# Splitting the attention result straight out of PSUM, in a kernel of linear attention and two MLPs

## The chip, the cores and the metric

The kernel runs on one core of a Trainium2 chip. The metric is the device time of one execution, in microseconds; the median of several executions counts. Times in the profile are those of one execution that the hardware profiler recorded.

## What is computed

An attention with a decaying state runs over 4 sequences of 768 steps, with 8 heads of 48 dimensions. Its output, as 3072 tokens of 384 numbers, goes through two MLPs of 2048 hidden units. The first has a clamped square as its activation, the second a sigmoid gate.

```python
for t in range(S):
    cur = np.einsum('bhd,bhe->bhde', u[None] * kt, vt)
    y[:, :, t] = np.einsum('bhd,bhde->bhe', rt, state + cur)
    state = wt[:, :, :, None] * state + np.einsum('bhd,bhe->bhde', kt, vt)
x = y.transpose(0, 2, 1, 3).reshape(B * S, H * D)

h = x @ w_in                                   # first MLP
g = np.where(h >= 1, h, np.where(h <= -1, 0.0, (h + 1) ** 2 / 4))
x = g @ w_out
h = x @ w2_in                                  # second MLP
out = (h / (1.0 + np.exp(-1.702 * h))) @ w2_out
```

## The kernel before

**Attention.** The 3072 tokens are cut into 24 windows of 128. `window(n)` is a generator that issues one window's instructions in about a dozen pieces, with a `yield` between them. A window loads its inputs (`rk`, `rkn`, `vn`, `lt`), runs two scans of the decay on VectorE (L433 and L435), multiplies and masks on GpSimd, ScalarE and VectorE, and does four groups of small matmuls: the transposes `tp`, the scores `sc`, the state `kv` and the result `yt`. At its end ScalarE copies the result `yt` from PSUM into `xr` in SBUF (L533). The four heads' pairs stand in four column blocks; six small DMAs (L536) move pieces of the fourth block into unused partitions of the other three, so that three blocks of 128 rows are left. Then ScalarE rounds `xr` into `xh` (L547), and VectorE (first six windows) or GpSimd (the other eighteen) forms the rest, `xl = xr - xh` (L550). `xr` has one buffer.

**MLPs.** Eight token tiles of 384, three windows each, go through the first MLP and then the second. One step `f` of a tile does nine matmuls of 128x384 into `hp` (L664: three of `xh` by `whi`, three of `xl` by `whi`, three of `xh` by `wlo`), the activation, and, three steps later, nine matmuls into three accumulators `acc` (L673, in the second MLP L682). Sixteen steps make a tile. The activation of the first MLP is three instructions: VectorE clamps `hp` to -1..1 (L701), ScalarE squares (L702), VectorE takes the maximum with `hp` (L714). ScalarE then rounds to `gh` (L695), and GpSimd or VectorE forms `gl` (L689).

**Weights.** They arrive as 64-bit numbers, in 32 pieces for the first MLP (`wst`, four buffers). Each piece costs two VectorE instructions (`ct` in PSUM, then `wt`), a ScalarE conversion (`wb`), an addition on GpSimd, a rounding on ScalarE (`whi`) and, from the eleventh piece on, a subtraction for `wlo` (L177), in turn on VectorE and GpSimd. The first ten pieces are converted before the first step.

**What sets the order.** Everything up to the end of the first tile (16 steps) is put in order by a scheduler, which may run an instruction earlier than it is written if it has a higher rank. The conversions inside the first tile are issued under `hooks["prio"](CP1)`, which gives them the rank `CP1`. From the second tile on, the order is the one in which the code is written: each step calls the attention's generators in turn, so that the windows of the next tile are spread over the steps of this one. A window whose last yielded value is `"x"` is held until its tile is at most one ahead of the tile that is running. Before, that yield stood ahead of the rounding into `xh`. DMAs are issued by SyncE (SP), in order.

The names that matter below: `xr`, `xh`, `xl` and the lines L533 to L550; `relu2_a` (L701, L702), `relu2_b` (L714); `split_x2`, which makes the second MLP's `xh` and `xl`; `ALT`, the choice of the activation's form in the first `ALT_N` tiles; `CP1`.

Of the kernel before, what the change touches and what calls it, by code (L numbers as in the profile page):

```python
# [9 lines left out]
F32 = mybir.dt.float32  # L10
F32R = mybir.dt.float32r
# [11 lines left out]
W = 128  # L23
# [15 lines left out]
TN = 384  # L39
# [12 lines left out]
LO0 = 'p'  # L52
LO1 = 'dg'
PUT = 1
ALT = (0,)
ALT_N = 1
N0 = 10
PRIO = True
# [4 lines left out]
F0 = 0  # L63
WP0 = 400
CP0 = 300
CP1 = 3000
MAXW = 6
GAP1 = 8
CHECK_LATE = True
# [30 lines left out]
def fast_path(st, tc, rkw_t, nat, v_l, w1, w2, u, out, x2_d, w2_d, flag_i, force):  # L100
# [121 lines left out]
            nc.scalar.activation(out=whi[f][q], in_=wf, func=AF.Copy)  # L222
            late.append((i, wf))

    xh, xl = {}, {}
    x2_t = {}
    accs = {}
    gq = {}
# [17 lines left out]

    def split_x2(i):
        x2 = x2_t.pop(i)
        h_ = p2.tile([128, KD, TN], F32R, tag="xh", name="x2h")
        l_ = p2.tile([128, KD, TN], F32R, tag="xl", name="x2l")  # L250
        nc.vector.tensor_copy(h_, x2)
        nc.vector.tensor_tensor(out=l_, in0=x2, in1=h_.bitcast(F32), op=ALU.subtract)
        xh[1, i], xl[1, i] = h_, l_
# [15 lines left out]
    def step(s):  # L269
        if s < NS:  # L270
            l, i, f, t0, n = where(s)
            last = l == 0 and i == len(TILES) - 1
            slots = l == 0 and not last
            if l == 0 and f == 0:
                cur[0] = i
            if l == 0 and i == 0:
                with hooks["prio"](CP1):
                    while nconv[0] < min(NPC, 2 * f + 2 + AHEAD):
                        conv_w1()
                    if nconv[0] == NPC:  # L280
                        conv_w1()
            hp = pools["h"][s % len(pools["h"])].tile([128, 512], F32, tag="h", name="hp")
            gemm1(nc, hp, n, xh[l, i], xl[l, i], f, win, whi, wlo)
            if l == 0 and ALT[f % len(ALT)] and i < ALT_N:
                t = relu2_c(nc, p2, hp, n, (None, nc.gpsimd, nc.vector)[ALT[f % len(ALT)]])
            else:
                t = (relu2_a, swish_a)[l](nc, p2, hp, n)
        if s - 1 in gq:
# [61 lines left out]
    with ExitStack() as sa:  # L350
# [65 lines left out]
        def window(n):  # L416
# [80 lines left out]
            yield from idle(GAPS[1])  # L497
            if PUT == 2 and not first:
                put(carry.pop())
            kvt = ps_s.tile([128, NC2, NP, D], F32, tag="s", name="kv")  # L500
            kv = [kvt[:, c] for c in range(1 if last else NC2)]

# [26 lines left out]
                carry.append(upd(1))  # L529
            yield from idle(GAPS[2])  # L530
            mm_y(1)
            xr = a2.tile([128, NP, W], F32, tag="xr", name="xr", bufs=1)
            nc.scalar.activation(out=xr, in_=yt, func=AF.Copy)  # L533
            for hh in range(2):
                for q in range(3):
                    nc.sync.dma_start(out=xr[64 * hh + D:64 * hh + 64, q, :], in_=xr[64 * hh + 16 * q:64 * hh + 16 * q + 16, 3, :])  # L536
            yield
            sq = vn.rearrange("p m h d -> p (m h d)")
            nc.scalar.activation(out=sq, in_=sq, func=AF.Square, accum_out=stat[:, n, 2:3])
            if n + 2 < NW:  # L540
                load_v(n + 2)
            yield "x"
            if off == 0:
                xh[0, ti] = p2.tile([128, KD, TN], F32R, tag="xh", name="xh")
                xl[0, ti] = p2.tile([128, KD, TN], F32R, tag="xl", name="xl")
            o = xh[0, ti][:, :, off:off + W]
            nc.scalar.activation(out=o, in_=xr[:, 0:KD, :], func=AF.Copy)  # L547
            if n >= XL_N:
                yield
            (nc.vector if n < XL_N else nc.gpsimd).tensor_tensor(out=xl[0, ti][:, :, off:off + W], in0=xr[:, 0:KD, :], in1=o.bitcast(F32), op=ALU.subtract)  # L550
            yield

        def idle(n):
# [152 lines left out]
def relu2_c(nc, p2, hp, n, eng):  # L706
    t = p2.tile([128, TN], F32, tag="t", name="t", bufs=3)
    nc.scalar.activation(out=t[:, 0:n], in_=hp[:, 0:n], func=AF.Relu, bias=0.5, scale=0.5)
    eng.scalar_tensor_tensor(out=t[:, 0:n], in0=t[:, 0:n], scalar=1.0, in1=t[:, 0:n], op0=ALU.min, op1=ALU.mult)
    return t  # L710


# [166 lines left out]
```

## Time and profile before

| what | value |
|---|---|
| median of 3 executions | 1003.78 us (1003.73 to 1005.83) |
| profiled execution, its own time | 1002.71 us |
| span from its first to its last instruction | 1001.0 us |
| PE busy | 945.8 us (94%) |
| VectorE (DVE) busy | 562.0 us (56%) |
| ScalarE (ACT) busy | 538.2 us (54%) |
| GpSimd (POOL) busy | 393.4 us (39%) |

The shares are means over stages that differ. In forty slices of the span, PE is at 4 to 6 tenths in the first four and at nine from the fifth on, while VectorE is at nine in the third, fourth and fifth slice. So the table has to be read together with a table by stage, which is what the first group of rows below is. Durations of neighbouring instructions on one engine overlap by some hundredths of a microsecond, so where many follow each other it is their distance from start to start that adds up.

### The profile page before, as it was taken

The page shows a single profiled execution, that of the slowest core. Times are in us where ns is not written, and L with a number is a line of the kernel's source. Part 1 is how long each engine was busy: PE and PEld are TensorE (multiplying, and loading weights), DVE is VectorE, ACT ScalarE, POOL GpSimd, SP SyncE. Part 2 cuts the span into 40 slices and gives each one's busy share as a digit, 9 for nine tenths or more (in the row PEclk, how much of TensorE's full clock was granted, in tenths as well). Part 3 has the DMA queues.
Part 4 walks back from the last instruction along what each step waited for, and adds up shares of the span by engine and source line. Part 5 has one row for each costly group of instructions (what it writes and reads, how often), then busy time and mean ns, then how long its engine had stood idle before and what let it go on. Part 6 is the DMA issues. An engine that isn't in the chain of part 4 may idle for free.

```text
span 1001.0 us, 18691 instructions
## 1 busy us (share of the span) xinstructions
PE 945.8 (94%) x6976; PEld 906.6 (91%) x6976; DVE 562.0 (56%) x983; ACT 538.2 (54%) x1279; POOL 393.4 (39%) x416
## 2 busy tenths in 40 slices
PE   4656999999999999999999999999999999999997
PEld 2445889999999999999999999999999999999997
DVE  6899976776877767777745753323232323232321
ACT  4666545666666667665654565555455433333332
POOL 6788744555555456455432541111111111111111
PEclk8857999999999999999999999999999999999999
DMA  9886515445555445553203443322222101000000
GB/s 236 208 226 176 140 24 164 132 118 140 156 134 147 117 113 154 144 146 104 66 20 115 129 133 99 96 78 85 87 81 85 59 2 45 3 28 22 25 1 28
DMA packets 52228, 101.73 MB, mean 102 GB/s; under 512 B 8608, under 2 KB 31392, under 8 KB 52128
## 3 DMA queue, kind: packets, MB, share of 16 engines
q1 hardware_dynamic: 52128, 100.45, 35.8%
q8 instruction: 57, 0.93, 0.4%
q14 instruction: 43, 0.35, 0.1%
HBM read 83.51 MB, written 15.73 MB: 99 GB/s over the span
## 4 chain that ended last, share of the span: by engine, by line
PE 63%; DVE 13%; ACT 10%; DMA 5%; issue 5%; SPq 3%; POOL 0%; ACTq 0%; DVEq 0%
PE hp L664 29%; PE acc L682 20%; PE acc L673 10%; SPq L536 3%; DVE pi L433 2%; DMA rk<-rkw_t 2%; DMA xr<-xr 2%; ACT gh L695 2%; DVE t L714 2%; ACT ra L472 2%; DVE ra L489 2%; ACT t L702 2%; DVE pi L435 1%; PE kv L508 1%; PE yt L514 1%
## 5 line engine op out<-in xcount | busy, mean ns | idle before, releaser
L689 POOL TENSOR_TENSOR gl<-t,gh 128x384 fp32r<-128x384 f32 x128 | 132.5, 1035 | 497.0 <-ACT gh L695 465.5
L695 ACT ACTIVATE gh<-t 128x384 fp32r<-128x384 f32 x256 | 134.1, 524 | 171.6 <-DVE t L714 93.4
L725 DVE TENSOR_TENSOR t<-t,hp 128x384 f32<-128x384 f32 x128 | 70.9, 554 | 218.6 <-ACT t L720 218.1
L720 ACT ACTIVATE t<-hp 128x384 f32<-128x384 f32 x128 | 62.8, 491 | 145.8 <-PE hp L664 145.8
L673 PE MATMUL acc<-gl,whi 128*128 128x384 f32 x384 | 131.2, 342 | 2.5 <-DVE gl L689 2.5
L673 PE MATMUL acc<-gh,whi 128*128 128x384 f32 x384 | 131.7, 351 | 0.8 <-ACT ev L263 0.3
L673 PE MATMUL acc<-gh,wlo 128*128 128x384 f32 x384 | 130.2, 339 | 0.0
L682 PE MATMUL acc<-wlo,gh 128*128 128x384 f32 x384 | 129.7, 338 | 0.0
L682 PE MATMUL acc<-whi,gh 128*128 128x384 f32 x384 | 129.5, 337 | 0.0
L682 PE MATMUL acc<-whi,gl 128*128 128x384 f32 x384 | 129.3, 337 | 0.0
L689 DVE TENSOR_TENSOR gl<-t,gh 128x384 fp32r<-128x384 f32 x128 | 75.4, 589 | 63.5 <-ACT gh L695 62.8
L702 ACT ACTIVATE t<-t 128x384 f32<-128x384 f32 x128 | 66.4, 519 | 65.7 <-DVE t L701 65.4
L714 DVE TENSOR_TENSOR t<-t,hp 128x384 f32<-128x384 f32 x128 | 70.2, 548 | 54.0 <-ACT t L702 52.5
L664 PE MATMUL hp<-xh,whi 128*128 128x384 f32 x384 | 91.9, 348 | 3.2 <-DVE t L714 3.2
L664 PE MATMUL hp<-xl,whi 128*128 128x384 f32 x384 | 89.3, 341 | 5.0 <-DVE xl L550 5.0
L701 DVE TENSOR_SCALAR t<-hp 128x384 f32<-128x384 f32 x128 | 70.4, 550 | 39.9 <-PE hp L664 39.6
L664 PE MATMUL hp<-x2h,whi 128*128 128x384 f32 x384 | 88.8, 339 | 0.0
L664 PE MATMUL hp<-xh,wlo 128*128 128x384 f32 x384 | 88.7, 339 | 0.0
L664 PE MATMUL hp<-x2l,whi 128*128 128x384 f32 x384 | 88.5, 339 | 0.0
L664 PE MATMUL hp<-x2h,wlo 128*128 128x384 f32 x384 | 88.1, 337 | 0.0
L673 PEld LDWEIGHTS acc<-gh,whi 128*128 128x128 f32 x384 | 72.2, 189 | 5.0 <-ACT ev L263 2.3
L673 PEld LDWEIGHTS acc<-gl,whi 128*128 128x128 f32 x384 | 72.6, 189 | 3.0 <-DVE gl L689 2.6
(108 smaller groups left out, 1849.1 us busy)
## 6 DMA issues: line engine op xcount, KB each, us to landing
wst<-w SPq DMA_DIRECT2D x96, 384.0 KB, 3.3
rk<-rkw_t SPq DMA_DIRECT2D x48, 288.9 KB, 5.0
rkn<-nat SPq DMA_DIRECT2D x24, 384.0 KB, 4.8
lt<-v_l SPq DMA_DIRECT2D x48, 128.0 KB, 3.7
w_d<-wt SPq DMA_DIRECT2D x32, 192.0 KB, 4.3
w2f<-w_d SPq DMA_DIRECT2D x32, 192.0 KB, 2.5
vn<-nat SPq DMA_DIRECT2D x24, 192.0 KB, 3.4
x_d<-ev SPq DMA_DIRECT2D x24, 192.0 KB, 2.2
```

What stands on the lines that cost most here:

```text
L433: nc.vector.tensor_tensor_scan(out=rr[:, WW:0:-1], data0=ws[:, WW:0:-1], data1=one_s[:, WW:0:-1], initial=0.0, op0=ALU.mult, op1=ALU.max)
L536: nc.sync.dma_start(out=xr[64 * hh + D:64 * hh + 64, q, :], in_=xr[64 * hh + 16 * q:64 * hh + 16 * q + 16, 3, :])
L664: nc.tensor.matmul(out=hp[:, 0:n], lhsT=win(a, f, kk), rhs=b[:, kk, 0:n], start=(i == 0), stop=(i == 3 * KD - 1))
L673: nc.tensor.matmul(out=acc[j][:, 0:n], lhsT=wout(a, f, j * 128, 128), rhs=b[:, 0:n], start=(f == 0 and i == 0), stop=(f == KF - 1 and i == 2))
L682: nc.tensor.matmul(out=o[:, 0:DM], lhsT=a[:, j * 128:(j + 1) * 128], rhs=wout(b, f, 0, DM), start=(f == 0 and i == 0), stop=(f == KF - 1 a ...
L689: eng.tensor_tensor(out=gl[:, 0:n], in0=t[:, 0:n], in1=gh[:, 0:n].bitcast(F32), op=ALU.subtract)
L695: nc.scalar.activation(out=gh[:, 0:n], in_=t[:, 0:n], func=AF.Copy)
L701: nc.vector.tensor_scalar(t[:, 0:n], hp[:, 0:n], scalar1=-1.0, scalar2=1.0, op0=ALU.max, op1=ALU.min)
L702: nc.scalar.activation(out=t[:, 0:n], in_=t[:, 0:n], func=AF.Square, bias=0.5, scale=0.5)
L714: nc.vector.tensor_tensor(out=t[:, 0:n], in0=t[:, 0:n], in1=hp[:, 0:n], op=ALU.max)
L720: nc.scalar.activation(out=t[:, 0:n], in_=hp[:, 0:n], func=AF.Sigmoid, scale=1.702)
L725: nc.vector.tensor_tensor(out=t[:, 0:n], in0=t[:, 0:n], in1=hp[:, 0:n], op=ALU.mult)
```

## The change

The window no longer has `xr`. ScalarE copies `yt` from PSUM directly into the rounded half of a joint tile `xx`, all four column blocks of it, and VectorE subtracts that half from `yt`, still in PSUM, into the other half. The six small DMAs then move both halves at once. The rounding and the subtraction that stood behind them are gone, for all windows. The yield of `"x"` moves up, ahead of the `kv` matmuls. The second MLP's pair comes from the same joint tile.

In the first tile (`ALT = (1,)`, `ALT_N = 1`) the activation's clamp and square become three ScalarE instructions, of which the first reads `hp`; VectorE keeps only the maximum (`relu2_b`, unchanged). `CP1` becomes 0: the conversions inside the first tile have no rank of their own.

```diff
-ALT = (0,)
+ALT = (1,)
-CP1 = 3000
+CP1 = 0
...
-        h_ = p2.tile([128, KD, TN], F32R, tag="xh", name="x2h")
-        l_ = p2.tile([128, KD, TN], F32R, tag="xl", name="x2l")
+        x = p2.tile([128, 2, NP, TN], F32R, tag="xx", name="xx2")
+        h_, l_ = x[:, 0, 0:KD], x[:, 1, 0:KD]
...
-                t = relu2_c(nc, p2, hp, n, (None, nc.gpsimd, nc.vector)[ALT[f % len(ALT)]])
+                t = relu2_d(nc, p2, hp, n)
...
+            yield "x"
             kvt = ps_s.tile([128, NC2, NP, D], F32, tag="s", name="kv")
...
-            xr = a2.tile([128, NP, W], F32, tag="xr", name="xr", bufs=1)
-            nc.scalar.activation(out=xr, in_=yt, func=AF.Copy)
+            if off == 0:
+                x = p2.tile([128, 2, NP, TN], F32R, tag="xx", name="xx")
+                xx[ti], xh[0, ti], xl[0, ti] = x, x[:, 0], x[:, 1]
+            o, ol = (xx[ti][:, q, :, off:off + W] for q in range(2))
+            nc.scalar.activation(out=o, in_=yt, func=AF.Copy)
+            nc.vector.tensor_tensor(out=ol, in0=yt, in1=o.bitcast(F32), op=ALU.subtract)
+            x = xx[ti][:, :, :, off:off + W].bitcast(F32)
             for hh in range(2):
                 for q in range(3):
-                    nc.sync.dma_start(out=xr[64 * hh + D:64 * hh + 64, q, :], in_=xr[64 * hh + 16 * q:64 * hh + 16 * q + 16, 3, :])
+                    nc.sync.dma_start(out=x[64 * hh + D:64 * hh + 64, :, q, :], in_=x[64 * hh + 16 * q:64 * hh + 16 * q + 16, :, 3, :])
...
-            yield "x"
-            if off == 0:
-                xh[0, ti] = p2.tile([128, KD, TN], F32R, tag="xh", name="xh")
-                xl[0, ti] = p2.tile([128, KD, TN], F32R, tag="xl", name="xl")
-            o = xh[0, ti][:, :, off:off + W]
-            nc.scalar.activation(out=o, in_=xr[:, 0:KD, :], func=AF.Copy)
-            if n >= XL_N:
-                yield
-            (nc.vector if n < XL_N else nc.gpsimd).tensor_tensor(out=xl[0, ti][:, :, off:off + W], in0=xr[:, 0:KD, :], in1=o.bitcast(F32), op=ALU.subtract)
...
+def relu2_d(nc, p2, hp, n):
+    t = p2.tile([128, TN], F32, tag="t", name="t", bufs=3)
+    nc.scalar.activation(out=t[:, 0:n], in_=hp[:, 0:n], func=AF.Relu, bias=0.5, scale=-0.5)
+    nc.scalar.activation(out=t[:, 0:n], in_=t[:, 0:n], func=AF.Relu, bias=1.0, scale=-1.0)
+    nc.scalar.activation(out=t[:, 0:n], in_=t[:, 0:n], func=AF.Square)
+    return t
```

The scheduler's order moves with it. On VectorE, the subtraction for window 2 (windows are counted from 0; window 2 is the last that the first tile needs) stood behind both scans of window 5, whose input is `rk_164`. Before:

```order
L433 SCALAR_TENSOR_TENSOR pi<-rk_164,one_s 128x516
L653 TENSOR_SCALAR ct<-wst 128x384
L460 TENSOR_REDUCE bb<-rkn 128x8
L434 RECIPROCAL seed<-pi 128x4
L441 TENSOR_TENSOR rk_164<-rk_164,pi 128x512
L655 SCALAR_TENSOR_TENSOR wt<-wst,ct 128x384
L435 SCALAR_TENSOR_TENSOR pi<-rk_164,seed 128x516
L550 TENSOR_TENSOR xl<-xr,xh 128x3x128
L177 TENSOR_TENSOR wlo_0_126<-wt,whi_0_94 128x384
```

In the changed kernel it stands one window earlier, between the scans of window 4 (`rk_163`); the rows now:

```order
L433 SCALAR_TENSOR_TENSOR pi<-rk_163,one_s 128x516
L652 SCALAR_TENSOR_TENSOR wt<-wst,ct 128x384
L177 TENSOR_TENSOR wlo_0_120<-wt,whi_0_88 128x384
L434 RECIPROCAL seed<-pi 128x4
L441 TENSOR_TENSOR rk_163<-rk_163,pi 128x512
L538 TENSOR_TENSOR xx<-yt,xx 128x4x128
L650 TENSOR_SCALAR ct<-wst 128x384
L435 SCALAR_TENSOR_TENSOR pi<-rk_163,seed 128x516
L177 TENSOR_TENSOR wlo_0_122<-wt,whi_0_90 128x384
```

So the subtraction moved up by about one window's work on VectorE, reads `yt` in PSUM, and the small DMAs now come after it. On SP, the six DMAs of window 2 stood between loads of weights; before:

```order
L140 DMA wst<-w 128x768
L536 DMA xr<-xr 16x128
L140 DMA wst<-w 128x768
L536 DMA xr<-xr 16x128
L140 DMA wst<-w 128x768
L536 DMA xr<-xr 16x128
L400 DMA rk_164<-rkw_t 48x1541 x2
L536 DMA xr<-xr 16x128 x2
L140 DMA wst<-w 128x768
L536 DMA xr<-xr 16x128
```

In the changed kernel three loads stand ahead of them and none between:

```order
L140 DMA wst<-w 128x768 x3
L542 DMA xx<-xx 16x2x128 x5
L400 DMA rk_164<-rkw_t 48x1541 x2
L542 DMA xx<-xx 16x2x128
L394 DMA rkn<-nat 128x768
```

The same six DMAs are issued, each with two halves, without a load of weights among them. On ScalarE the first tile's first activations stand among conversions and a window's work (`pi`, `ra`); before:

```order
L459 ACTIVATE pi,stat<-pi 128x2x516
L472 ACTIVATE ra_1029<-rk_164 64x512
L472 ACTIVATE ra_1030<-rk_164 64x512
L702 ACTIVATE t<-t 128x384
L654 ACTIVATE wb<-wst 128x384
L168 ACTIVATE whi_1_97<-wt 128x384
L547 ACTIVATE xh<-xr 128x3x128
L702 ACTIVATE t<-t 128x384
```

Now, at the same activations:

```order
L712 ACTIVATE t<-hp 128x384
L713 ACTIVATE t<-t 128x384
L714 ACTIVATE t<-t 128x384
L712 ACTIVATE t<-hp 128x384
L651 ACTIVATE wb<-wst 128x384
L168 ACTIVATE whi_1_95<-wt 128x384
L713 ACTIVATE t<-t 128x384
L493 ACTIVATE rk_163,stat<-rk_163 128x512
L494 ACTIVATE rk_163,stat<-rk_163 128x512
L692 ACTIVATE gh<-t 128x384
```

Each step has three instructions in a chain on ScalarE in place of one, the first of them waits for PE's `hp`, and other work stands between the second step's.

## Rows read from the trace of the kernel before

**Rows 1.** Table by stage: busy us and instructions of each engine, granted clock, DMA.
```profile
core 0: us, PE busy (x) PEld busy (x) DVE busy (x) ACT busy (x) POOL busy (x), PEclk, DMA share, GB/s
...
61.57:90.54 28.97, 12.85 (x134) 11.19 (x134) 28.53 (x38) 15.94 (x38) 23.42 (x22) 0.57 0.67 189
90.54:130.66 40.12, 36.05 (x294) 31.45 (x294) 39.22 (x64) 25.05 (x60) 30.28 (x31) 0.96 0.63 158
130.66:160.24 29.58, 29.58 (x197) 27.46 (x197) 17.39 (x34) 14.52 (x30) 12.57 (x13) 1.00 0.08 21
160.24:520.00 359.76, 356.16 (x3263) 337.57 (x3262) 262.04 (x471) 231.76 (x583) 188.21 (x207) 1.00 0.47 127
```

**Rows 2.** Timeline, 76 to 85 us: start, duration, engine, instruction, [idle before it <- releaser].
```profile
76.64 2.54 POOL L464 TENSOR_SCALAR_AFFINE_SELECT ra<-bb 64x512 f32<-64x512 f32 x2
...
78.66 4.94 DVE L550 TENSOR_TENSOR xl<-xr,xh 128x384 fp32r<-128x384 f32 x1
...
82.19 0.98 POOL L436 TENSOR_TENSOR rkn<-rkn 128x384 f32<-128x384 f32 x1
...
83.62 0.60 ACT L533 ACTIVATE xr<-yt 128x512 f32<-128x512 f32 x1 [6.01 <-DVE xl L550]
...
83.65 1.33 PE L664 MATMUL hp<-xl,whi 128*128 128x384 f32 x3 [5.01 <-DVE xl L550]
```

**Rows 3.** Groups by line on VectorE, 61.57 to 130.66 us: xcount | busy, mean ns.
```profile
L177 DVE TENSOR_TENSOR wlo<-wt,whi 128x384 fp32r<-128x384 f32 x9 | 9.6, 1063 | 0.0
...
L550 DVE TENSOR_TENSOR xl<-xr,xh 128x384 fp32r<-128x384 f32 x4 | 7.1, 1782 | 0.0
...
L441 DVE TENSOR_TENSOR rk<-rk,pi 128x512 f32<-128x512 f32 x4 | 3.0, 747 | 0.0
```

**Rows 4.** Timeline of VectorE: the distance of neighbours, and the first and ninth maximum.
```profile
88.23 0.54 DVE L653 TENSOR_SCALAR ct<-wst 128x384 int32<-128x384 int32 x1
88.69 0.54 DVE L701 TENSOR_SCALAR t<-hp 128x384 f32<-128x384 f32 x1
...
90.54 0.53 DVE L714 TENSOR_TENSOR t<-t,hp 128x384 f32<-128x384 f32 x1
...
130.66 0.53 DVE L714 TENSOR_TENSOR t<-t,hp 128x384 f32<-128x384 f32 x1
```

**Rows 5.** Single lines, VectorE: durations in ns, min/median/max (the first up to 150 us).
```profile
L714 DVE TENSOR_TENSOR t<-t,hp x15: 522/541/556, 90.5 to 148.5; 128x384 f32<-128x384 f32 x15
...
L441 DVE TENSOR_TENSOR rk<-rk,pi x24: 655/684/1449, 15.3 to 498.0; 128x512 f32<-128x512 f32 x24
...
L489 DVE COPY_PREDICATED ra<-mask,sc x48: 719/741/761, 24.2 to 508.5; 64x512 f32<-64x512 int32 x48
```

**Rows 6.** Timeline of SP's issues and of VectorE's scan of window 4.
```profile
44.69 6.46 SPq L536 DMA_DIRECT2D xr<-xr  x6
51.26 1.48 SPq L140 DMA_DIRECT2D wst<-w  x3
52.84 0.83 SPq L400 DMA_DIRECT2D rk<-rkw_t  x2
...
61.57 2.60 DVE L433 TENSOR_TENSOR_SCAN pi<-rk,one_s 128x516 f32<-128x516 f32 x1 [1.43 <-DMA rk<-rkw_t]
```

**Rows 7.** Timeline of PE: start of the first tile's step 8; one window's `kv` matmuls.
```profile
122.24 0.80 PE L664 MATMUL hp<-xh,whi 128*128 128x384 f32 x3
...
166.63 1.06 PE L508 MATMUL kv<-vn,ktok 64*48 64x48 f32 x32
```

**Rows 8.** Timeline of ScalarE: two neighbours.
```profile
93.23 0.51 ACT L168 ACTIVATE whi<-wt 128x384 fp32r<-128x384 f32 x1
93.65 0.51 ACT L695 ACTIVATE gh<-t 128x384 fp32r<-128x384 f32 x1
```

**Rows 9.** Who PE waited for, 160.24 to 520 us: us in total, times, longest.
```profile
PE yt L514 <- DVE ra L489: 1.4, 4, 0.4
PE kv L508 <- ACT ktok L486: 1.3, 2, 0.7
```

More of the change, by code (lines that the diff above doesn't have):

```diff
@@ L223, in fetch_w2 @@
             late.append((i, wf))
-    xh, xl = {}, {}
+    xh, xl, xx = {}, {}, {}
     x2_t = {}
```

## The prediction, made before the changed kernel was run

> **What bounds the kernel now.** I read the table by stage first. In 130.66 to 160.24 us and in 160.24 to 520 us PE is busy 29.58 of 29.58 and 356.16 of 359.76 us at the full clock [rows 1]: there PE is the bound, and all that the change can win there is the 3.6 us in which PE idles. From 61.57 to 90.54 us PE is busy 12.85 of 28.97 us at a granted clock of 0.57, and VectorE 28.53; from 90.54 to 130.66 us VectorE is busy 39.22 of 40.12 us, ScalarE 25.05, GpSimd 30.28 [rows 1]. So ahead of 130 us the bound is VectorE: it holds the windows' scans and masks, two instructions for each piece of weights, and the first tile's clamps and maxima, and PE waits for them. Since PE's work is not changed, the end moves by as much as VectorE's chain through the first tile moves.
>
> Inside that chain I looked for durations far above the usual. The `xl` of window 2, a 128x384 subtraction, is 4.94 us long. GpSimd ran one instruction after the other from 76.64 to 83.17 us, and the subtraction ended 0.4 us after that run. PE's first `hp` waited 5.01 us for it, and ScalarE's next `xr`, which has one buffer, 6.01 us [rows 2]. Others of its kind (two operands in SBUF) are long as well: nine `wlo` take 1063 ns on average [rows 3], although a usual 128x384 instruction takes 0.54 us and starts 0.46 us after its neighbour [rows 4]. The maximum L714, which reads PSUM as one operand, never took over 556 ns in this stage [rows 5].
>
> **The change, part by part.** I mark the chain by two instructions of VectorE that both orders have: the scan L433 of window 4, at 61.57 us, and the maximum of the ninth step (f = 8), at 130.66 us [rows 4, 6]. Between them I counted the instructions in the two orders; what isn't named is equal.
>
> *Clamps.* Nine L701 go from VectorE: 9 x 0.46 = -4.1 us [rows 4].
>
> *Conversions without rank.* At window 4's scan the new order has converted two pieces fewer than the old, and at the ninth maximum two more: three more `ct` and four more `wt` lie between the marks, 7 x 0.46 = +3.2 us [rows 4], and two more `wlo`, at their mean of 1.06 us +2.1 us [rows 3]. One `rk` product (L441, 0.75 us) moves out: -0.75 us [rows 3]. These conversions are only moved; all 32 are done by the ninth step in the new order, so what follows has none.
>
> *xl from PSUM.* Four L550 with 7.1 us in all [rows 3] become four subtractions of 128x512 that read `yt` in PSUM. No such row exists. The nearest are L441, 128x512 without a wait at 655 ns, and L714, which reads PSUM at 541 ns for 384 columns [rows 5]; both say 0.55 to 0.75 us, and I take 0.66: 2.6 us, so -4.5 us. Of the 7.1 us, 4 x 0.46 = 1.8 is work and 5.3 was waiting. If that wait is only inherited by the next subtraction or scan with two SBUF operands, the part comes to +0.8 us instead. I take a quarter as inherited (+1.3): a wait lasts until GpSimd's run ends, and in the new order `ct`, `wt` and the masks, which read PSUM or one tensor, fill part of that time. The maxima and `ct` of rows 4 stay at 0.54 us beside a GpSimd that is busy three quarters of the time.
>
> The Trainium skill ("SBUF — State Buffer", section "Who interferes with whom") says that a VectorE instruction with two SBUF inputs is locked out by a GpSimd instruction that reads SBUF, for the whole of it, and one with a single SBUF input isn't. By that rule alone the new subtraction never waits, and `wlo`, `gl` and scans go on waiting; the rows above agree with both halves. It prices this part at an estimated -4.5 us if nothing is inherited.
>
> *The start of the chain.* Window 4's scan waited 1.43 us for its `rk` DMA, which SP issued at 52.84 us behind six small DMAs (6.46 us of issuing) and three loads [rows 6]. In the new order three small DMAs and two loads stand between the `lt` loads and this `rk`, but the small DMAs now wait for VectorE's subtraction too, which I place some 5 us later than the old copy. Bounds: 0, and -2.2 us if three of the six (3.2 us) fall away less a wait of 1 us. I take -1.
>
> *Sum to the mark:* -4.1 + 3.2 + 2.1 - 0.75 - 4.5 + 1.3 - 1.0 = -3.75 us, between +1.3 (everything inherited, no earlier scan) and -6.3 (nothing inherited, the scan 2.2 us earlier).
>
> *What PE still has to do.* Window 6's `kv` matmuls were partly done in the first tile, and now the `"x"` yield holds them until the second. By the eleventh step's `hp` (f = 10), which waits for that ninth maximum because the first tile has two `hp` banks, PE has about two thirds of one window's `kv`, 0.7 us of 1.06 [rows 7], left to do in addition: +0.7. Net -3 us.
>
> *Steady part, 160 to 520 us.* Eighteen windows: ScalarE loses one instruction each (0.42 us from start to start [rows 8]), GpSimd one, VectorE gains 0.66 us (12 us on an engine that is busy 262 of 360). In each, VectorE now also stops at the subtraction until ScalarE has copied `yt`; behind it stand the maximum of the same step and its `gh`. The matmuls that need them come three steps later, so I cost it at nothing; if that cover is gone, PE waits. PE's waits there, mostly for masks and `ktok`, are 0.2 to 0.7 us each [rows 9]. I take 0, from -2 to +2. The last window of a tile has its second `yt` in step 12 of 16 in place of 11, so the six DMAs keep some four steps.
>
> *To the median.* Span 1001.0 - 3.0 = 998.0. The profiled execution is 1.7 us longer than its span and 1.07 us under the median, so 1002.71 - 3.0 + 1.07 = **1000.8 us**.
>
> **The rivals.**
>
> *ScalarE becomes the bound of the first tile (slower).* From the first maximum to the ninth ScalarE is busy 25.05 of 40.12 us [rows 1]. Nine steps bring 18 more instructions (7.6 us at 0.42 [rows 8]), five more pieces of weights fall between (`wb` and `whi`, 4.2 us), and three `xh` go (-1.3): about 36 us. Every maximum now waits for a chain of three on an engine in which conversions and windows stand between. From the order I expect the first maximum at 83.5 us in place of 90.54 (to that mark the new order has one conversion (0.9 us), two masks (1.5 [rows 5]), two clamps (0.9) and the 4.94 us less, two of the new subtractions (1.3) and 1 us of inherited waiting more, and starts 1 us earlier), and the net is zero when the stretch to the ninth takes 46.5 us (130.66 - 0.7 - 83.5). VectorE alone needs about 43.5 there. If ScalarE keeps half of its present idle 15 us as waiting, the stretch is 43.5 us and nothing is lost; if it keeps all of it, 51 us: +4.5, so 1008.3 us. The rival decides between the two, from 46.5 us on; I price it at half of the way, 1006 us. Against it: part of those 15 us was waiting for the very clamps that go.
>
> *The wait moves (same).* The run of GpSimd's instructions is as long as before, and the next `wlo` or scan waits in place of `xl`: +4.0 of the 5.3 us on top of my quarter gives 1000.8 + 4.0 = 1004.8 at worst, and half of that 1002.8 us. For it: the long `wlo`. Against it: PSUM readers fill the gap.
>
> *More than the sum.* The first `hp` can start when window 2's small DMAs have landed. They stood between loads of weights and then waited for `xl`; now they don't. If conversions behind the first step are hidden under PE's work, the lead of 7 us at the first maximum stays: 1003.8 - 7 = 996.8 us.
>
> **How the numbers follow.** A measurement of this kernel can tell about 0.2%, 2 us, from no change; the border of faster is 1001.8 us. The forecast, with its own range 998 to 1003, has a chance of 0.50, of which 0.40 lies under 1001.8. ScalarE as the bound: 0.20, nearly all of it slower. The moved wait: 0.22, of which 0.16 same, 0.04 slower and 0.02 faster. More than the sum: 0.08. Together faster 0.50, same 0.28, slower 0.22. The range that leaves out 0.2: from 995.5 to 1007 us.
>
> **What would show it.** Right: the new subtraction at 0.6 to 0.75 us with no long one among them; window 4's scan at 60 to 61.5 us; PE's first full `hp` before 79 us where the long `xl` held it until 83.65 [rows 2]; the first maximum near 83.5 and the ninth near 127 us; step 8's `hp` ahead of 122.24 us [rows 7]. The clamps' place taken by ScalarE near 0.9 busy from 83 to 127 us. The forecast is wrong if VectorE shows idle time in that stretch that ends with a ScalarE instruction, if `wlo` or scans have grown to 2 us and more, or if PE idles over 5 us between 160 and 520 us.

## The result: 1% faster, and where it came from

The changed kernel takes 993.52 us, the median of five executions (990.96 to 997.57), against 1003.78 us of the kernel before: a ratio of 0.9901 with a 95% interval from 0.9884 to 0.9919. The forecast was 1000.8 us with a range down to 995.5. So the sign was right, and the gain of 10.3 us is more than three times the 3 us predicted. The profiled execution took 990.96 us and is the fastest of the five; its span is 989.2 against 1001.0 us. A second profile of the changed kernel (991.93 us, from the run "changed kernel as it is" below) has the marks of the table, from window 4's scan to step 112, within 0.6 us of these.

The instructions that split the two programs into the same stretches show where the 11.8 us of span lie. PE's steps are counted from the first tile on, 16 to a tile: step 18 is the third of the second tile, step 112 the first of the eighth. The timeline has these four rows of PE, the first two from the kernel before, the others from the changed one (start, duration, instruction):

```profile
158.49 0.69 PE L664 MATMUL hp<-xh,whi 128*128 128x384 f32 x3
...
532.74 0.69 PE L664 MATMUL hp<-xh,whi 128*128 128x384 f32 x3
```
```profile
153.01 0.80 PE L661 MATMUL hp<-xx,whi 128*128 128x384 f32 x3
...
520.92 0.87 PE L661 MATMUL hp<-xx,whi 128*128 128x384 f32 x4
```

VectorE's rows of the changed kernel that answer to [rows 4, 6]: window 4's scan, the first and the ninth maximum, and two of the new subtractions.

```profile
57.29 1.23 DVE L433 TENSOR_TENSOR_SCAN pi<-rk,one_s 128x516 f32<-128x516 f32 x1 [1.60 <-DMA rk<-rkw_t]
...
61.30 0.68 DVE L538 TENSOR_TENSOR xx<-yt,xx 128x512 fp32r<-128x512 f32 x1
...
77.18 0.66 DVE L538 TENSOR_TENSOR xx<-yt,xx 128x512 fp32r<-128x512 f32 x1
...
80.58 0.54 DVE L719 TENSOR_TENSOR t<-t,hp 128x384 f32<-128x384 f32 x1
...
126.17 0.56 DVE L719 TENSOR_TENSOR t<-t,hp 128x384 f32<-128x384 f32 x1 [0.71 <-ACT t L714]
```

| stretch | before, us | after, us | difference | forecast |
|---|---|---|---|---|
| start to window 4's scan | 61.57 | 57.29 | -4.28 | -1.0 |
| scan to the ninth maximum | 69.09 | 68.88 | -0.21 | -2.75 |
| ninth maximum to step 18 | 27.83 | 26.84 | -0.99 | +0.7 |
| step 18 to step 112 | 374.25 | 367.91 | -6.34 | 0 |
| step 112 to the end | 468.26 | 468.28 | 0 | 0 |

The ninth maximum is where it was forecast (126.17 for "near 127"), but by other terms than those of the sum, so that agreement is luck; and more than half of the gain is in the steady part, which the forecast had put at nothing. The table by stage of the changed kernel, cut at the same instructions (columns as in [rows 1]):

```profile
57.29:80.58 23.29, 13.73 (x178) 11.33 (x174) 22.41 (x34) 14.36 (x35) 20.30 (x19) 0.65 0.73 211
80.58:126.17 45.59, 39.84 (x294) 36.12 (x295) 39.33 (x68) 35.31 (x85) 39.02 (x38) 0.82 0.71 192
126.17:153.01 26.84, 26.84 (x203) 25.89 (x202) 10.94 (x22) 16.57 (x34) 6.84 (x7) 1.00 0.10 20
153.01:520.92 367.91, 367.82 (x3348) 351.33 (x3345) 289.43 (x501) 232.03 (x582) 188.85 (x195) 1.00 0.45 124
```

The last of these stretches in the kernel before:

```profile
158.49:532.74 374.25, 370.65 (x3345) 352.02 (x3345) 268.29 (x483) 238.59 (x597) 192.28 (x211) 1.00 0.45 124
```

In the steady part PE idled 3.60 us before and idles 0.09 us now, with the same number of weight loads (3345); the table of waits has no row for PE there any more, and [rows 9] are gone. From window 4's scan to the ninth maximum VectorE's busy time fell from 67.75 us [rows 1] to 61.74, more than the 2.75 us of the sum, but its idle time rose from 1.34 to 7.14 us. The list of its waits from 58 to 131 us says for whom (us in total, times, longest):

```profile
DVE pi L433 <- DMA rk<-rkw_t: 4.1, 3, 1.9
DVE t L719 <- ACT t L714: 3.3, 3, 2.2
DVE pi L433 <- ACT t L713: 2.0, 1, 2.0
DVE wlo L177 <- ACT whi L168: 0.9, 1, 0.9
```

### The profile page after: what moved, and what is told of

The parts are those of the page before. It is cut to its first block, busy times and chain, and to the rows that moved or that the text cites. A ratio compares the mean times of both kernels' runs of the same rounds, so it can differ in the third digit from the quotient of the medians.

```text
span 989.2 us, 18602 instructions
## 1 busy us (share of the span) xinstructions
PE 947.3 (96%) x6976; PEld 909.6 (92%) x6976; DVE 568.6 (57%) x985; ACT 542.2 (55%) x1287; POOL 387.4 (39%) x398
## 4 chain that ended last, share of the span: by engine, by line
PE 88%; DMA 4%; DVE 4%; issue 1%; ACT 1%; POOL 0%; SPq 0%; DVEq 0%; ACTq 0%; POOLq 0%
PE hp L661 40%; PE acc L670 21%; PE acc L679 20%; DMA rk<-rkw_t 3%; PE sc L484 2%; PE yt L515 2%; PE kv L509 2%; DVE pi L433 1%; PE tp L479 1%; DMA wst<-w 1%; DMA xx<-xx 0%; DVE ct L650 0%; DVE wlo L177 0%; DVE pi L435 0%; PE cps L173 0%
## 5 line engine op out<-in xcount | busy, mean ns | idle before, releaser
L686 POOL TENSOR_TENSOR gl<-t,gh 128x384 fp32r<-128x384 f32 x128 | 137.7, 1076 | 482.8 <-ACT gh L692 457.0
L661 PE MATMUL hp<-xx,whi 128*128 128x384 f32 x1536 | 317.3, 342 | 5.6 <-DVE t L719 3.5
L661 PEld LDWEIGHTS hp<-xx,whi 128*128 128x128 f32 x1536 | 273.4, 190 | 8.0 <-DVE t L719 4.2
L661 PE MATMUL hp<-xx,wlo 128*128 128x384 f32 x768 | 176.9, 338 | 0.0
L661 PEld LDWEIGHTS hp<-xx,wlo 128*128 128x128 f32 x768 | 138.7, 189 | 0.0
L686 DVE TENSOR_TENSOR gl<-t,gh 128x384 fp32r<-128x384 f32 x128 | 77.7, 607 | 51.7 <-ACT gh L692 50.3
L699 ACT ACTIVATE t<-t 128x384 f32<-128x384 f32 x112 | 58.2, 520 | 56.6 <-DVE t L698 56.2
L698 DVE TENSOR_SCALAR t<-hp 128x384 f32<-128x384 f32 x112 | 61.6, 550 | 29.2 <-PE hp L661 28.9
L670 PEld LDWEIGHTS acc<-gh,wlo 128*128 128x128 f32 x384 | 72.6, 189 | 0.0
L679 PEld LDWEIGHTS acc<-whi,gl 128*128 128x128 f32 x384 | 72.1, 188 | 0.0
```

The costliest lines, as they stand in the source:

```text
L661: nc.tensor.matmul(out=hp[:, 0:n], lhsT=win(a, f, kk), rhs=b[:, kk, 0:n], start=(i == 0), stop=(i == 3 * KD - 1))
L670: nc.tensor.matmul(out=acc[j][:, 0:n], lhsT=wout(a, f, j * 128, 128), rhs=b[:, 0:n], start=(f == 0 and i == 0), stop=(f == KF - 1 and i == 2))
L679: nc.tensor.matmul(out=o[:, 0:DM], lhsT=a[:, j * 128:(j + 1) * 128], rhs=wout(b, f, 0, DM), start=(f == 0 and i == 0), stop=(f == KF - 1 a ...
L686: eng.tensor_tensor(out=gl[:, 0:n], in0=t[:, 0:n], in1=gh[:, 0:n].bitcast(F32), op=ALU.subtract)
L698: nc.vector.tensor_scalar(t[:, 0:n], hp[:, 0:n], scalar1=-1.0, scalar2=1.0, op0=ALU.max, op1=ALU.min)
L699: nc.scalar.activation(out=t[:, 0:n], in_=t[:, 0:n], func=AF.Square, bias=0.5, scale=0.5)
```

## The experiments

The change has four parts: the path of `xh` and `xl`, the place of the `"x"` yield (I call it the gate), the clamps on ScalarE, and the rank. Ratios are to the kernel before on the same chip.

**Clamps and rank.** Path and gate alone, with clamps and rank as before:

```diff
-ALT = (1,)
+ALT = (0,)
-CP1 = 0
+CP1 = 3000
```

> The changed kernel with the clamps back on VectorE and the rank back on the conversions: the new path of xh and xl, and the gate, are all that is left of the change. Theory G with the prediction's sum for the first tile: the gate gives 5 to 7 us and the subtraction from PSUM with the earlier chain 3 to 5, so 992 to 996 us; clamps and rank then carry next to nothing, since their -4.1 and +4.5 us cancel. Rival C: the clamps carry the first tile's gain: 997 to 999 us.

Measured: 993.89 us, 0.9909 (0.9895 to 0.9923), the changed kernel's own time. The two edits that held four of the sum's terms carry nothing together that is clear of the noise. Each was then undone by itself. With the rank back (`CP1 = 3000`):

> The changed kernel with the rank of 3000 back on the conversions inside the first tile. Theory: the conversions are only moved, PE has room for the first steps anyway; the first maximum comes later than 80.6 us and the ninth at 126 to 128, time 993 to 996 us. Rival: without the rank conversions had fallen into time that VectorE idles in, and with it they hold up the first tile's steps again: 997 us and more.

995.85 us, 0.9932 (0.9916 to 0.9948). With the clamps back on VectorE (`ALT = (0,)`):

> The changed kernel with the first tile's clamps back on VectorE, conversions still without rank. Theory from the two runs so far (with rank and clamps both back 993.9, with the rank alone back 995.9): the clamps cost VectorE 4.1 us up to the ninth maximum, but PE has a reserve by then and gets back a part: 994 to 997 us. Rival: the three relus in a row on ScalarE cost as much as the clamps: 992.5 to 994 us.

991.64 us, 0.9876 (0.9859 to 0.9892). Both expectations of this run had it slower or the same. It was measured again beside the changed kernel:

> The changed kernel with the first tile's clamps back on VectorE, measured beside the changed kernel. Theory: three relus in a row on ScalarE cost more than nine clamps on VectorE, 1 to 3 us less than the changed kernel. Rival: the two differ by less than 1 us.

> The changed kernel as it is, on the chip of the next runs. 0.989 to 0.992 of the kernel before.

991.24 us and 0.9881 (0.9865 to 0.9897) with the clamps back, 994.19 us and 0.9918 (0.9905 to 0.9931) for the changed kernel. In the four combinations the relus cost 1.9 to 3.0 us with the rank and without, and the missing rank gains 1.7 to 2.7 us: the two cancel. The relus' cost is clear of the noise in the repeated pair, whose intervals don't meet; the rank's gain is so only just, in one of its pairs (0.9909 against 0.9876). The version with clamps on VectorE is the fastest of all that were run.

The traces show where VectorE's time went, though not the whole of the difference. The first table row is this version's, from window 4's scan (59.80) to the ninth maximum (123.58); the rows under it are its waits of VectorE.

```profile
59.80:123.58 63.78, 48.80 (x434) 42.36 (x430) 61.46 (x99) 37.30 (x86) 51.99 (x50) 0.79 0.64 181
```
```profile
DVE pi L433 <- DMA rk<-rkw_t: 1.7, 2, 1.5
DVE pi L433 <- ACT xx L537: 1.5, 1, 1.5
DVE t L698 <- PE hp L661: 0.2, 1, 0.2
```

VectorE is busy 61.46 us here and 61.74 in the changed kernel (22.41 + 39.33 in the table above), so the nine clamps that left were filled up: in the changed kernel three more `ct`, four more `wt`, two more `wlo` and two more masks lie in the stretch. What differs is the stretch itself, 63.78 against 68.88 us: with the relus VectorE sits idle for 7.14 us in place of 2.32, and the maximum waits for L714, the square that ends ScalarE's chain of three. But little of these 5 us reaches the end. With the clamps on VectorE window 4's scan is 2.5 us later, from the ninth maximum to step 18 PE takes 30.08 us in place of 26.84, and step 18 comes at 153.66 us against 153.01 (in the repeated pair at 152.43 against 152.83). So the profiles leave open where the 2 to 3 us of the medians arise.

**The gate.** Moved up in the kernel before, nothing else:

```diff
+            yield "x"
             kvt = ps_s.tile([128, NC2, NP, D], F32, tag="s", name="kv")
...
-            yield "x"
+            yield
             if off == 0:
```

> The kernel before with the yield of x moved up ahead of the kv matmuls, and nothing else. Theory G: the gate is worth half of the gain; without it PE starts window 6's kv and yt one by one among the first tile's last steps (18 changes between large and small matmuls in 122 to 158 us of the trace before, 3.1 us over the plain work) and waits once or twice in a tile for ktok or ra. It gives 5 to 7 us back, so 997 to 999 us, and the ninth maximum stays near 130.7 us. Rival P: the steady part gains because ScalarE and GpSimd have one instruction less in each window; then the gate alone gives 1003 to 1004.5 us. The prediction's own term for it was +0.7 us.

1021.99 us, 1.0183 (1.0168 to 1.0198): neither theory. Step 18 is 0.4 us late, as before; from there to step 112 it loses 21.2 us. And moved down in the changed kernel, behind the second `yt` group:

> The changed kernel with the yield of x moved down, from ahead of the kv matmuls to behind the second yt group, so that kv and yt of a tile's first window are again done one tile earlier. Theory G: the waits of PE for ktok and ra come back in the steady part, and so do changes between large and small matmuls in the first tile: 997 to 1000 us. Rival P: it stays at 992.5 to 994.5 us.

1001.28 us, 0.9972 (0.9958 to 0.9985). Step 18 comes 6.7 us later than in the changed kernel, and 18 to 112 takes 372.36 us in place of 367.91. So the gate is worth nearly 8 us, but only together with the path. To part its two places, it was moved down for windows 9 to 23 alone (`if n < 9:` ahead of the upper yield, `if n >= 9:` ahead of the lower):

> The changed kernel with the gate ahead of kv for windows 0 to 8 and behind the second yt group for windows 9 to 23: the first tile and its successor stand as in the changed kernel, the rest of the steady part as in the run with the late gate. Theory: the gate acts in two places. The first tile keeps its lead (step 18 some 5.5 us ahead of the kernel before), the steady part loses what it had gained by the gate, 3 to 5 us: 996 to 999 us. Rival: all of the gate's worth is in the first tile, and it stays at 992 to 995 us.

998.04 us, 0.9946 (0.9931 to 0.9961), 4.5 us above the changed kernel: the gate acts in both. Its waits of PE from 192 to 530 us are of the kind that [rows 9] had:

```profile
PE kv L510 <- ACT ktok L486: 2.5, 2, 1.4
PE acc L673 <- ACT ev L263: 1.9, 3, 0.7
```

Is it the holding of a window, or only that the moved yield puts one more slot between a window's scores and its `kv`? The late gate got that slot in another way, and so did the kernel before:

```diff
-GAPS = (1, 1, 1)
+GAPS = (1, 2, 1)
```

> The run with the late gate, with one more idle slot between a window's scores and its kv matmuls, which is what the moved yield does for a window that it doesn't hold. Theory S: in the steady part it is the slot alone that takes PE's waits for ktok and ra away, so it gains 3 to 5 us on the late gate's 1001.3: 996.5 to 998.5 us, with the first tile as slow as there. Rival H: it is the holding of a tile's first window, and the time stays at 1000.5 to 1002 us.

> The kernel before with one more idle slot between scores and kv, nothing else. Theory S: PE's waits for ktok and ra in the steady part (2.7 us in all, more with the short ones) go, 999 to 1002 us. Rival: with the old path a later yt only brings the wait for the single xr, as it did with the moved gate alone: 1005 us and more.

1001.25 us, 0.9975 (0.9963 to 0.9986), no gain, and 1013.64 us, 1.0100 (1.0084 to 1.0116). The slot alone is not it. In the late gate's run it did take PE's waits for `ktok` ahead of `kv` away, but waits of 2.8 us ahead of `sc` came in their place, and step 18 came 3.2 us later.

**The phase of the windows.** The run with the gate alone had one more difference: with its yields a window is two slots longer than in the changed kernel (one in the first six windows), and PE's `kv` stands at other steps (21, 26, 33, 37 in place of 22, 27, 33, 38). Two runs cross path and phase. The kernel before with the gate up, the old yields taken out, which gives the changed kernel's steps on PE:

```diff
-            yield "x"
             if off == 0:
...
-            if n >= XL_N:
-                yield
```

> The kernel before with the yield of x moved up and two yields fewer in a window's end, so that on PE the windows' scores, kv and yt stand at the very steps of the changed kernel (scores at 20, 25, 30, 36; kv at 22, 27, 33, 38); xr, its single buffer, xl from SBUF, clamps and rank are as before. Theory phase: in the steady part the gain is the phase of the windows against the steps, not the path: from step 26 to step 112 it gains 3 to 5 us on the kernel before; the first tile, where VectorE is the bound, gains nothing or 1 us: 998 to 1001 us. Rival: the old path can't use the early gate at all, and waits for the single xr make it slow again: 1010 us and more.

And the changed kernel with the other phase, by two yields at a window's end (one in the first six windows) and no other instruction:

```diff
+            if n >= XL_N:
+                yield
+            yield
```

> The changed kernel with two yields more at a window's end, so that PE's order has the phase of the run with the gate alone (scores at 19, 24, 30, 35; kv at 21, 26, 33, 37), with the path from PSUM. Theory phase: the copy of yt and the next window's scores fall into one slot again, PE waits in each tile, and the steady part loses much of what the gate alone lost, 10 to 20 us: 1003 to 1014 us. Rival: the loss of the gate alone came from the single xr and the old path; then the time stays at 992 to 996 us.

1054.27 us, 1.0505 (1.0490 to 1.0519), and 1031.02 us, 1.0272 (1.0255 to 1.0288). So the good phase does not help the old path: it costs 50 us there, as the rival had it. The other phase costs the changed kernel 37 us, more than expected, 34 of them between steps 18 and 112. PE's waits in that second run, 190 to 561 us, and their place in the timeline, once in each tile:

```profile
PE sc L484 <- DVE xx L538: 8.9, 5, 1.8
PE tp L479 <- DVE us L521: 7.9, 5, 1.6
PE yt L515 <- DVE lt L521: 4.1, 4, 1.3
```
```profile
226.98 0.63 PE L479 MATMUL tp<-ident,rk 128*128 128x128 f32 x4 [1.57 <-DVE us L521]
229.39 1.15 PE L484 MATMUL sc<-rk 48*64 48x64 f32 x32 [1.78 <-DVE xx L538]
```

One window's result and the next one's `tp` and `sc` now meet in one slot, and share two banks of PSUM. The waits sum to 21 us. Another 7.8 us lie between neighbouring large matmuls: the same 1641 pairs take 301.7 us from start to start here and 294.0 in the changed kernel, and no wait is noted among them. PE's lower clock behind such pauses (last section) fits that; that it is all of it is not shown. In the run with the old path at the good phase the wait is another one. PE waits for the copy of the accumulators (six times, 23.6 us in all), and ScalarE stands in front of it at `xh`, which waits for the small DMAs (ScalarE's rows under PE's):

```profile
240.55 0.69 PE L671 MATMUL acc<-gh,whi 128*128 128x384 f32 x1 [4.29 <-ACT ev L263]
```
```profile
239.59 0.52 ACT L547 ACTIVATE xh<-xr 128x384 fp32r<-128x384 f32 x1 [2.89 <-DMA xr<-xr]
240.02 0.85 ACT L263 ACTIVATE ev<-acc 128x384 f32<-128x384 f32 x2
```

The new path has nothing on ScalarE or VectorE behind the small DMAs; only PE's `hp` waits for them, a tile later. That this is what lets the early gate pay is argued from these rows; no run changed it alone.

**PSUM or SBUF as the source.** The subtraction of the first six windows reads an SBUF copy, which ScalarE makes in addition:

```diff
+            ys = yt
+            if n < XL_N:
+                ys = a2.tile([128, NP, W], F32, tag="xr", name="xr", bufs=1)
+                nc.scalar.activation(out=ys, in_=yt, func=AF.Copy)
-            nc.vector.tensor_tensor(out=ol, in0=yt, in1=o.bitcast(F32), op=ALU.subtract)
+            nc.vector.tensor_tensor(out=ol, in0=ys, in1=o.bitcast(F32), op=ALU.subtract)
```

> The changed kernel with one more ScalarE copy of yt into SBUF in the first six windows, from which VectorE subtracts there: the subtraction has two operands in SBUF again, all else is as in the changed kernel. Theory: these six subtractions wait for the end of GpSimd's runs, some of them last 2 to 5 us where they last 0.67 now, and the time is 2 to 5 us above the changed kernel's 993.5: 995.5 to 998.5 us. Rival: the long one in the trace of before was a chance meeting; then the subtractions stay under 1.4 us and the time under 995 us.

1002.38 us, 0.9993 (0.9984 to 1.0002). Neither theory nor rival: the time rose by 9 us, yet no subtraction was as long as 2 us. Its durations (min/median/max in ns), and under them the 24 of the changed kernel:

```profile
L542 DVE TENSOR_TENSOR xx<-xr,xx x6: 659/709/1340, 32.8 to 110.7; 128x512 fp32r<-128x512 f32 x6
```
```profile
L538 DVE TENSOR_TENSOR xx<-yt,xx x24: 659/691/693, 30.8 to 509.2; 128x512 fp32r<-128x512 f32 x24
```

The same with the copy made and not used (`in0=yt`):

> The changed kernel with the additional copy of yt into SBUF in the first six windows, which nothing reads: the subtraction takes PSUM again. Theory order: the 9 us came from where the scheduler put window 4's rk load on SP (issued at 58.19 us with the copy and its use, at 51.39 in the changed kernel), behind fewer loads here; window 4's scan is back at 57 to 60 us, time 994 to 998 us. Rival source: they came from the subtraction waiting or being long in SBUF, then it is 993 to 994.5 us. Rival copy: ScalarE's copy itself costs them by holding the bank of yt, then it stays at 1000 to 1003 us though the scan is early.

1001.49 us, 0.9983 (0.9972 to 0.9995). So the source is worth 1 us or less, and an additional copy of 0.6 us per window costs 7 to 8 us. A part of it is seen at window 4's scan: it starts at 61.92 us with the copy alone and at 66.35 with its use, against 57.29. In both the scan waits for its `rk` load, as in [rows 6], which the scheduler has put later on SP; the first row is of the copy alone, the two others of the copy with its use:

```profile
55.73 0.98 SPq L400 DMA_DIRECT2D rk<-rkw_t  x2
```
```profile
57.67 0.42 SPq L140 DMA_DIRECT2D wst<-w  x1
58.19 0.84 SPq L400 DMA_DIRECT2D rk<-rkw_t  x2
```

**A pair that failed.** The lower gate of the run above holds a bank of PSUM while it waits. To free it, the gate went behind the small DMAs, with a third buffer for `xx` and, to make room, the scratch of the weights' check in the tag `ev`; a second run had these with the gate up.

> The changed kernel with the gate behind the small DMAs, where a held window keeps no bank of PSUM, and with a third buffer of xx for it (the checking of weights takes its scratch from the tag ev to make room). Theory: a held window's bank was no part of the late gate's loss, and the time is that of the late gate, 1000 to 1002.5 us. Rival: the bank was the loss, and it is 993 to 997 us.

> The changed kernel with the third buffer of xx and the checking scratch in the tag ev, the gate where the change puts it. Theory: buffer and scratch cost nothing, 992 to 995.5 us, and the 8.8 us between the late gate with three buffers and the changed kernel belong to the gate. Rival: they cost up to 8 us themselves, 997 us and more.

1002.31 us, 0.9993 (0.9981 to 1.0004), and 1018.70 us, 1.0153 (1.0139 to 1.0166). In the second ScalarE waited 28.3 us for the DMAs that empty `ev` before it could write the scratch, so the rig itself costs time in the steady part and the pair decides nothing there. In the first tile, where the scratch isn't used, step 18 is 3.1 us earlier with the gate up.

## Why the forecast was right in sign and wrong in size

*The steady part, taken as 0 from -2 to +2: wrong, -6.34 us.* This is the step that failed. It looked at single waits, found each covered, left them as they were, and took the 3.6 us of PE's idle time as all that could be won. Two things were missed.

First, the yield of `"x"` was read as a hold for the first tile only; in each tile it also changes which pieces of two windows meet in one slot, and by the runs with other phases that is worth tens of microseconds. The waits that the forecast left in place went. Two of them, in the kernel before:

```profile
188.98 1.06 PE L508 MATMUL kv<-vn,ktok 64*48 64x48 f32 x32 [0.71 <-ACT ktok L486]
...
210.47 0.77 PE L514 MATMUL yt<-ra,lt 128*64 128x64 f32 x16 [0.36 <-DVE ra L489]
```

Second, these waits cost more than the idle time that the profile shows. From step 18 to step 112 both kernels have the same matmuls in the same number, 1692 large ones (128x384) and 17 windows' small ones, with the same number of changes between them. So the 6.34 us can be added up from the distances from start to start. The steps from a large matmul to `kv` sum to 6.22 us in the kernel before and 4.51 now, those from `kv` to `yt` to 3.25 and 0.94, those among `yt` to 15.91 and 15.27, and those between large ones, where PE waited for copies of the accumulators (`ev`), to 295.93 and 293.97. The other steps take 0.3 us more now. Only 3.5 us of this stood in the profile as idle time: a large matmul is recorded for 0.34 us, the next one starts 0.18 us after it (141.68 and 141.86 in the last rows of the next item), and a wait that fits into the overlap counts as busy. With the gate late again in the changed kernel the steps to `kv` are long again (7.87 us) and those from `sc` to a large matmul take 1.1 us more; the others stay short. So the gate took the waits for `ktok`, and the others went with the rest of the change; which part of it took them was not separated.

The weight loads (PEld) gave a sign of this room that the forecast passed over: from 160.24 to 520 us they were busy for 337.57 of 359.76 us, 94%, where PE stood at 99% [rows 1]; from step 18 to step 112 they were busy for 352.02 of 374.25 us before and 351.33 of 367.91 now, 95%. The Trainium skill ("Perfetto Trace Analysis", section "Identifying the Most-Contended Engine") says to judge how full TensorE is by the share of its weight loads and by the work it does, and not by its matmuls' busy time; the rows agree.

*PE's deferred `kv`, +0.7: wrong sign, -0.99 us.* The work did move behind the ninth maximum, but as one group of 32. Before, `kv` and `yt` stand one at a time among the accumulations at the end of the first tile: 18 changes between large and small matmuls from step 8 to step 18, in 36.25 us that count as busy. At 0.176 us for a large matmul and 0.03 for a small one, both from start to start in undisturbed rows, the 177 large and 62 small ones of this stretch are worth 33.0 us; the other 3.2 are an estimate of what the changes cost. In the changed kernel there are 4 changes, and the same estimate gives 0.6 us. The first rows are of before, the last of the changed kernel:

```profile
136.63 0.68 PE L673 MATMUL acc<-gh,whi 128*128 128x384 f32 x3
137.24 0.24 PE L508 MATMUL kv<-vn,ktok 128*48 128x48 f32 x1
137.25 0.27 PE L514 MATMUL yt<-ra,lt 128*64 128x64 f32 x1
137.32 0.21 PE L508 MATMUL kv<-vn,ktok 128*48 128x48 f32 x1
137.36 0.22 PE L514 MATMUL yt<-ra,lt 128*64 128x64 f32 x1
137.51 0.44 PE L673 MATMUL acc<-gl,whi 128*128 128x384 f32 x1
137.79 0.34 PE L673 MATMUL acc<-gh,wlo 128*128 128x384 f32 x1
```
```profile
141.15 0.69 PE L670 MATMUL acc<-gh,whi 128*128 128x384 f32 x3
141.68 0.34 PE L670 MATMUL acc<-gl,whi 128*128 128x384 f32 x1
141.86 0.34 PE L670 MATMUL acc<-gh,wlo 128*128 128x384 f32 x1
```

Three matmuls and a change take 0.61 us where three take 0.53, and from the first large one behind the small ones to the next it is 0.28 where 0.17 to 0.18 is usual.

*The start of the chain, -1 from -2.2 to 0: -4.28 us, outside its bounds.* The bounds counted SP's issuing alone (the `rk` load goes out 1.45 us earlier, 51.39 for 52.84). They left out how long the load takes to land. Before, it went out behind three loads of weights and the scan could start 7.9 us after its issue had ended (52.84 + 0.83 to 61.57 [rows 6]). Now it is 4.9 us (52.36 to 57.29), with the weights' loads 2.6 us ahead:

```profile
46.29 2.51 SPq L140 DMA_DIRECT2D wst<-w  x2
49.32 1.95 SPq L542 DMA_DIRECT2D xx<-xx  x3
51.39 0.97 SPq L400 DMA_DIRECT2D rk<-rkw_t  x2
```

The runs with the copy agree: 5.2 us without a load of weights right ahead of it (56.71 to 61.92), 7.3 with one (59.03 to 66.35). So do the others: by the time at which the DMA landed it took 6.0 to 7.8 us from the end of the issue in the five runs with a load of weights right ahead, and 4.4 to 5.7 us in the other thirteen.

*Clamps -4.1, conversions +4.55: wrong in what they are worth.* By instructions both came as counted. But the conversions moved with the relus, not with the rank (in the four combinations 15 or 16 `ct` lie in the stretch with clamps and 18 with relus, whatever the rank), and with the relus VectorE waits 4.8 us more (7.14 for 2.32), for which the sum had no term.

*xl from PSUM, -4.5 and +1.3 inherited: right in size, nothing inherited.* Four subtractions cost 2.7 us (4 x 0.67). The Trainium skill ("SBUF — State Buffer", section "Who interferes with whom") has a VectorE instruction with one SBUF operand run free of GpSimd's reads; 24 subtractions between 659 and 693 ns agree, and so do all 312 of the thirteen runs that subtract from PSUM alone (657 to 695 ns), while in the same runs single scans took up to 4.80 us and one `wlo` 3.94, with two operands in SBUF. That the operand in SBUF was the whole reason for the 4.94 us is not shown: with it back the longest subtraction took 1.34 us.

*The signs named.* Right were the subtractions (all 0.66 to 0.69 us), the first full `hp` before 79 us (73.65), step 8's `hp` (120.36, ahead of 122.24) and no `wlo` or scan of 2 us (in the second profile of the changed kernel one scan took 2.92). Wrong were window 4's scan (60 to 61.5), the first maximum (83.5) and ScalarE near 0.9 busy: it was 35.31 of 45.59 us, 0.77. And VectorE's idle time that ends with ScalarE did show, which the forecast had named as a sign against itself.

*The rivals.* ScalarE as the bound of the first tile came true in part: the stretch from the first maximum to the ninth took 45.59 us, just short of the 46.5 from which it would have cost the earlier start, and by the medians the relus cost 2 to 3 us against clamps on VectorE. "More than the sum" described the first maximum (10 us earlier) but not the way the rest of the gain came. The moved wait did not show in this profile: `wlo` averaged 901 ns, before 1063 [rows 3].

*What stays open.* How the gate's worth divides: from 3.1 to 6.7 us in the first tile, by two pairs of runs that put the late gate at different places, and some 4.5 in the steady part. Why one phase is good was not derived, only that it is, and only for the new path. Why the medians put the clamps on VectorE ahead is open. And the idle copy costs 11.1 us up to step 18 in its profiled execution: 4.6 us are the late `rk` load, 2.7 lie between the scan and the ninth maximum and 3.8 behind it, and their causes were not followed.

## What to carry to other kernels

Where generators or queues interleave stages by slots, a yield that is moved or removed is an edit of its own: list which pieces now meet in a slot on each engine, and try a slot more or less before believing a gain or a loss. Take "busy" for an upper bound of an engine's work: multiply instructions by the distance from start to start of undisturbed ones, and the difference is the most that can still be won. Undo each part of a change alone; here two parts cancelled within the noise, and the version without one of them (clamps on VectorE, 991.2 to 991.6 us) beats both kernels.

## What the runs showed of the hardware

A change between the large matmuls and the small ones cost PE 0.1 to 0.2 us (an estimate from the first tile's end: 3.2 us for 18 changes, 0.6 for 4), inside what the profile counts as busy. It seems to go with the shape of the weights and not with the number of columns moved: the step from large matmuls to the transposes `tp`, whose weights are 128x128 too and which move 128 columns in place of 384, costs nothing extra, and the step on to `sc` does. In the kernel before (two large ones 0.35 us, then three transposes at 0.11 and a step of 0.20):

```profile
159.72 0.51 PE L664 MATMUL hp<-xh,wlo 128*128 128x384 f32 x2
160.07 0.60 PE L479 MATMUL tp<-ident,rk 128*128 128x128 f32 x4
160.60 1.15 PE L484 MATMUL sc<-rk 48*64 48x64 f32 x32
```

The Trainium skill ("TensorEngine Tiling (Array Packing)", section "Key Properties") says that a change of the tile mode drains the engine. No row names the mode of a matmul, so these rows agree with it but don't show the cause.

In the run with the other phase a pause of PE cost more than itself. The granted clock was 0.91 from 215 to 235 us, around pauses of 0.8 to 1.8 us, and 1.00 on either side; the next matmuls are slower, as on the lower of the two levels (1.2 GHz): 0.32 us from row to row where 0.18 is usual.

```profile
230.75 0.34 PE L673 MATMUL acc<-gl,whi 128*128 128x384 f32 x1
230.93 0.46 PE L673 MATMUL acc<-gh,wlo 128*128 128x384 f32 x1
231.18 0.52 PE L673 MATMUL acc<-gh,whi 128*128 128x384 f32 x1
231.50 0.52 PE L673 MATMUL acc<-gl,whi 128*128 128x384 f32 x1
```

A load of about 0.6 MB (`rk`) landed 4.4 to 5.7 us after its issue had ended when no load of weights went out right ahead of it, and 6.0 to 7.8 us after it when one did. A subtraction on VectorE with one operand in PSUM took 657 to 695 ns in all 312 cases.
